# Attention scores by single heads and half tiles in quarters of TensorE's array, with first and second heads in separate PSUM banks

## The chip, the cores and the metric

One Trainium2 chip, one of its cores. The metric is the device time of one execution in microseconds (us). The kernel has an attention stage (about the first 147 us of the span) and behind it a mixture-of-experts stage; the change touches the attention stage alone.

## The reference, cut to what matters

```python
def _attn_ref(q, k, v):                       # 8 batches, 8 heads, 576 queries, 64 values a head
    k_p = k.reshape(B, H, Sp, 8, D).mean(axis=3)      # keys and values pooled by 8: Sp = 72
    v_p = v.reshape(B, H, Sp, 8, D).mean(axis=3)
    scores = scale * np.matmul(q, k_p.transpose(0, 1, 3, 2))
    scores = scores - np.max(scores, axis=-1, keepdims=True)
    attn = np.exp(scores)
    attn = attn / (np.sum(attn, axis=-1, keepdims=True) + 1e-09)
    return np.matmul(attn, v_p)
...
```

The result, 4608 rows of 512 numbers, goes through a gate to one of 8 experts (two layers, 512 to 1024 to 512) and is added to itself; rows that a skip score leaves out stay as they are.

## The kernel before, in words

**Tiling.** The 4608 queries are 36 tiles of 128. A batch has 576 queries, which are four and a half tiles, so four of the 36 tiles (t = 4, 13, 22, 31) hold 64 queries of one batch and 64 of the next. All eight heads of a tile are worked on together, as four pairs g. The queries lie as `qts[..][:, t % QG, g, :]`: 128 partitions, of which 0 to 63 are the 64 dimensions of the pair's first head and 64 to 127 those of its second, by 128 queries.

**Scores (`scores`, L299 to L305).** The pooled keys of a batch lie in `kbd`, for each pair a block-diagonal matrix of 128 partitions by 144: the first head's 72 keys stand in partitions 0 to 63 and columns 0 to 71, the second head's in partitions 64 to 127 and columns 72 to 143, and the rest is zero. `keys` (L213, ScalarE) writes it. One matmul of a pair (L303, queries as the weights, 144 moving columns, 128 rows deep) gives both heads' scores. `scores(t, half)` does pairs 0 and 1 into one PSUM bank, `scores(t, 1)` pairs 2 and 3 into a second one. A tile of two batches does each matmul in two halves of 64 queries, each with its own batch's keys. All of it is fp32, and the trace shows each such matmul as two weight loads and two matmuls ("passes" below; a transpose is one). There are three banks for scores (`ps_s`, L169), so a tile's second bank is the one that the tile before used first.

**Softmax.** `least` (L309, VectorE) takes, bank by bank, the smallest of each head's negated scores. `exped` (L315, ScalarE) makes the exponentials, one instruction per head, four for each bank, into `e`.

**Values.** `turn_p` (L323, L324) transposes `e` on TensorE into one PSUM tile `pt` of which there is one; `turned_p` (L328, ScalarE) copies it to `pT` in one instruction; `values` (L341, L344) multiplies by the values into `o`, of which there is also one; `normalised` (L355 to L362, VectorE) divides by the sum and writes the rows `x`, which go out by DMA, and the gate's logits.

**The order** is written out by hand, since the stage is under a manual schedule: each engine does its instructions in the order in which the program emits them. In step t of the loop (L842 to L896) the steps that matter here are, in this order: copy `pT` of tile t-2 (L848), for a new batch copy its transposed values (`turned_v`, L267), divide tile t-3 (`normal`), scores of tile t (L856), smallest scores (L861), for a new batch the gate's products (`gates_pe`, L278), in some steps the routing's products (L397 to L401), exponentials of t (L874), values of t-2 (L875), transposes of t-1 (L877). Weight splits on ScalarE and VectorE, sums of values on GpSimd, loads and indirect writes are put in between by planners with costs and due steps; none of these is touched.

**The start** (L819 to L840) does the scores and exponentials of tiles 0 and 1, then the sums of the first batch's values on VectorE (`first_sums`, L239), the transposes and the `pT` of both tiles, the first batch's gate products and the scores of tile 2. The keys of the first batch come pair by pair: the loop at L740 sums one pair's keys on VectorE (`sum_k`, L208) and writes its two blocks on ScalarE (L213), so that the first tile's matmuls follow pair by pair.

Of the kernel before, what the change touches and what calls it, by code (L numbers as in the profile page):

```python
# [26 lines left out]
F32 = mybir.dt.float32  # L27
# [3 lines left out]
AF = mybir.ActivationFunctionType  # L31
# [5 lines left out]
B, H, S, HD, POOL = 8, 8, 576, 64, 8  # L37
SP = S // POOL
# [44 lines left out]
QG = 2  # L83
KO = 128 - SP
KL = SP - KO
GAP = 2 * KL
# [77 lines left out]
def attention(tc, nc, q, k, vm, vr, cf, wg, w1, w2, whi, wlo, out, c, pay, offs, table, near, bufs, late, early, mb, fin, cfs):  # L164
    with ExitStack() as ctx:
# [3 lines left out]
        ps_s = pool("ps_s", 3, space=PSUM)  # L169
# [14 lines left out]
        kbd = [third[:, i * n:i * n + n].rearrange("p (g k) -> p g k", g=4) for i in range(2)]  # L184
# [9 lines left out]
        halves = [slice(hh * 64, hh * 64 + 64) for hh in range(2)]  # L194
        kts, kps, vts, vss, lss, vTs, qts = {}, {}, {}, {}, {}, {}, {}
# [9 lines left out]
        def sum_k(b, g):  # L205
            if b not in kps:
                kps[b] = kp.tile([128, 4, SP], F32, name="kp")
            nc.vector.tensor_reduce(kps[b][:, g], kts[b][:, g], axis=AX.X, op=ALU.add)  # L208
# [56 lines left out]
        def turned_v(b, tp):  # L265
            vTs[b] = vT = vp.tile([128, 3, 128], F32, name="vT", bufs=1)
            nc.scalar.activation(vT, tp, AF.Copy)  # L267
# [7 lines left out]
        def gates_pe(b):  # L275
            vT = vTs.pop(b)
            for j in range(3):
                nc.tensor.matmul(gp[:, j * 36:j * 36 + 36], vT[:, j, :], wgs[:, j * 36:j * 36 + 36], start=True, stop=True)  # L278

        def gates_dve(b):  # L280
            nc.vector.tensor_tensor(vbd[b % 2].rearrange("p g (h c) -> p g h c", h=2)[:, :, :, HD:VA - 1],
                                    gp[:, 0:72].rearrange("p (g h c) -> p g h c", g=4, h=2),
                                    pair.unsqueeze(3).broadcast_to([128, 4, 2, 9]), ALU.mult)
            nc.vector.tensor_tensor(vl4[b % 3][0:n4, :, HD:VA - 1], gp[:n4, 72:108].rearrange("p (g c) -> p g c", g=4),
                                    left.unsqueeze(2).broadcast_to([n4, 4, 9]), ALU.mult)
# [8 lines left out]
        def parts(t):  # L294

            b0, b1 = t * 128 // S, (t * 128 + 127) // S
            return [(slice(0, 128), b0)] if b0 == b1 else [(slice(0, 64), b0), (slice(64, 128), b1)]

        def scores(t, half):  # L299
            sc = ps_s.tile([128, 512], F32, name="sc")[:, 0:4 * SP]  # L300
            for g in range(2):
                for sl, b in parts(t):
                    nc.tensor.matmul(sc[sl, g * 2 * SP:(g + 1) * 2 * SP], qts[t // QG][:, t % QG, half * 2 + g, sl],  # L303
                                     kbd[b % 2][:, half * 2 + g, :], start=True, stop=True)
            return sc  # L305

        def least(sc, mn, i):

            nc.vector.tensor_reduce(mn[:, i * 4:i * 4 + 4], sc.rearrange("p (h k) -> p h k", k=SP), axis=AX.X, op=ALU.min)  # L309

        def exped(e, sc, mn, i):
            ev = e[:, (4 * SP + GAP) * i:(4 * SP + GAP) * i + 4 * SP].rearrange("p (k g) -> p g k", g=2)
            for h in range(4):
                k0 = (h % 2 ^ i) * SP
                nc.scalar.activation(ev[:, h // 2, k0:k0 + SP], sc[:, h * SP:(h + 1) * SP], AF.Exp,  # L315
                                     bias=mn[:, 4 * i + h:4 * i + h + 1], scale=-1.0)

        def turn_p(e):
            for i in range(2):
                k0 = (4 * SP + GAP + 2 * KL) * i  # L320
                ev = e[:, k0:k0 + 256].rearrange("p (k g) -> p g k", g=2)
                for g in range(2):
                    nc.tensor.transpose(ptf[:, (2 * i + g) * 128:(2 * i + g) * 128 + 128], ev[:, g], ident)  # L323
            nc.tensor.transpose(ptf[:, 512:640], e[:, 256:384], ident)  # L324

        def turned_p():
            pT = ap.tile([128, 5, 128], F32, name="pT")
            nc.scalar.activation(flat(pT), ptf[:, 0:640], AF.Copy)  # L328
            return pT

        def values(t, pT, apart=False):
            if apart:
                os = [ps_s.tile([128, 512], F32, name="sc") for _ in range(2)]
            else:
                o = ps_o.tile([128, 2, 512], F32, name="o")
                os = [o[:, 0], o[:, 1]]
            for a, o_ in enumerate(os):
                ov = o_[:, 0:4 * VA].rearrange("p (g h c) -> p g h c", g=2, h=2)
                for g in range(2):
                    for sl, b in parts(t):  # L340
                        nc.tensor.matmul(o_[sl, g * 2 * VA:(g + 1) * 2 * VA], pT[:, 2 * a + g, sl], vbd[b % 2][:, 2 * a + g, :],  # L341
                                         start=(g == 0), stop=False)
                for sl, b in parts(t):
                    nc.tensor.matmul(ov[sl, :, 1, :], pT[:, 4, sl], vl4[b % 3][:, 2 * a:2 * a + 2, :], start=False, stop=True)  # L344
            return [o_.unsqueeze(1) for o_ in os] if apart else [o]
# [250 lines left out]
        class Queue:  # L596
# [18 lines left out]
            def exponentials(self):  # L615
                if self.held is EXPS:
                    self.step(True)
# [119 lines left out]
        o = ps_o.tile([128, 2, 512], F32, name="o")  # L737
# [52 lines left out]
        scs, es, pts, os_ = {}, {}, {}, {}  # L790
# [6 lines left out]
        def normal(t):  # L797
            nrm = normalised(t, os_.pop(t))
            next(nrm)
            routes.step()  # L800
            finish(nrm)
            routes.step()
            add_routes(t + 1)

        def softmax(t, sc):
            mn = ap.tile([128, H], F32, name="mn")
            for i in range(2):
                least(sc[i], mn, i)
            return mn

        def exponentials(t, sc, mn):
            es[t] = ebuf[t % 2]
            for i in range(2):
                exped(es[t], sc[i], mn, i)

        def constant_product():
            nc.tensor.matmul(o[:, 0, :], init[:, 0:128], init[:, 0:512], start=True, stop=True)
# [1 line left out]
        for t in range(2):  # L819
            now["t"] = t  # L820
            for f in loads.pop(t, ()):
                f()
            sc = [scores(t, i) for i in range(2)]
            exponentials(t, sc, softmax(t, sc))
        constant_product()
        first_sums()
# [7 lines left out]
        sum_k(1, 1)  # L834
        gates_pe(0)
        gates_dve(0)
        sc = [scores(2, i) for i in range(2)]
        mn = softmax(2, sc)
        sum_k(1, 2)
        gps.take(1)  # L840
# [1 line left out]
        for t in range(2, NT):  # L842
            now["t"] = t
            for f in loads.pop(t, ()):
                f()
            new = turns.get(t)
            if t > 3:
                pts[t - 2] = turned_p()  # L848
            if t > NT - TILES:
                xhigh()  # L850
            if new is not None:
                turned_v(new, tp)
            routes.exponentials()
            if t > 2:
                normal(t - 3)
                sc = [scores(t, i) for i in range(2)]  # L856
            if t == NT - 1:
                turn_p(es.pop(t - 1))
                pts[t - 1] = turned_p()
            if t > 2:  # L860
                mn = softmax(t, sc)  # L861
            if t == 3:
                sum_k(1, 3)
            if new is not None:
                gates_pe(new)
            if t > NT - TILES:
                xlow()
            if t == NT - 1:
                while routes.step():
                    pass  # L870
            else:
                routes.products()
            spent = act.take(t, 0.4 if new is not None else 0.0, 1)
            exponentials(t, sc, mn)  # L874
            os_[t - 2] = values(t - 2, pts.pop(t - 2))  # L875
            if 2 < t < NT - 1:
                turn_p(es.pop(t - 1))  # L877
            if t >= NT - TILES:
                assert not later
                if t == NT - TILES:  # L880
                    tx, steps = tile_steps()
                xhigh, xlow = tx(bufs["ring"][:, t - NT + TILES], t - NT + TILES, ps_s.tile([128, 512], F32, name="sc"))
            if new is not None:
                gates_dve(new)
            for hh in range(2) if t in (2, 3) else ():
                keys(1, hh, slice(0, 3) if t == 2 else slice(3, 4))
            busy = dve.take(t, 0.25 if new is not None else 0.0)
            act.take(t, spent)
            while t < NT - 1 and busy < (DVE if t < PICKED else DVEL) and routes.step():
                busy += 0.24  # L890
            later.pop(t, lambda: None)()
            if t == FILLS:
                gps.fill = clear
            gps.take(t)
            if t + 1 in turns:
                tp = turn_v(turns[t + 1])  # L896
# [883 lines left out]
```

## Time and profile before

| what | us |
|---|---|
| median of 3 runs (482.95, 485.91, 1611.41) | 485.91 |
| profiled execution, its own time | 483.38 |
| span of that profile | 481.3 |
| TensorE matmul busy, weight loads busy | 464.6, 417.1 |
| VectorE, ScalarE, GpSimd busy | 304.0, 225.7, 247.9 |

The span runs from the first to the last instruction of the program; 2.1 us of the execution's time lie around it. One of the three runs is far from the other two, so the lower two, 3 us apart, are what the profiled execution is to be held against. TensorE's granted clock is full speed in all 40 slices.

### The profile page before, as it was taken

To read this page: it belongs to the slowest core of one execution; us is meant where nothing else is said; L and a number is where in the kernel's file an instruction comes from. 1 tells how busy PE (TensorE), PEld (TensorE's weight loads), DVE (VectorE), ACT (ScalarE), POOL (GpSimd) and SP (SyncE) were. 2 spreads that over 40 slices of the span, in tenths; PEclk is the share of its full clock that TensorE was granted. 3 is DMA by queue.
4 is the path that set the end of the run, shared out by engine and by line. 5 is a ranking of instruction groups with operands and counts; after the bars stand their busy time and mean duration, and the time that the engine had idled before them with its cause. 6 is when DMAs were issued, how large, how long until landed. Compare 5 with 4: busy or idle time off the path is not lost. (4 is left out here: it accounts for less than half of the span.)

```text
span 481.3 us, 11187 instructions
## 1 busy us (share of the span) xinstructions
PE 464.6 (97%) x3043; PEld 417.1 (87%) x3044; DVE 304.0 (63%) x713; ACT 225.7 (47%) x578; POOL 247.9 (52%) x328
## 2 busy tenths in 40 slices
PE   7999999999999999999999998999999999999995
PEld 3799899989999879898989986989899898989894
DVE  5877888798788622579795667662846655343321
ACT  4678778888891201545463645512435241212110
POOL 4498499999998054433343525153443161515242
PEclk9999999999999999999999999999999999999999
DMA  8999999996931025689787496877577323322021
GB/s 278 396 394 392 345 360 338 362 337 212 327 113 68 11 54 190 207 260 325 217 320 239 124 325 231 303 235 257 189 238 255 101 88 109 128 65 88 22 87 42
DMA packets 52042, 103.88 MB, mean 216 GB/s; under 512 B 10031, under 2 KB 22959, under 8 KB 50336
## 3 DMA queue, kind: packets, MB, share of 16 engines
q1 hardware_dynamic: 40544, 78.18, 47.8%
q0 software_dynamic: 11456, 25.22, 14.9%
q8 instruction: 17, 0.28, 0.2%
q14 instruction: 25, 0.20, 0.1%
HBM read 80.85 MB, written 31.21 MB: 233 GB/s over the span
## 5 line engine op out<-in xcount | busy, mean ns | idle before, releaser
L1288 POOL DMA_INDIRECT out<-ring,slot x33 | 34.9, 1057 | 107.3 <-POOLq L1114 103.9
L315 ACT ACTIVATE e<-sc,mn 128x72 f32<-128x72 f32 x288 | 65.0, 346 | 7.2 <-DVE mn L309 6.8
L1520 ACT ACTIVATE hhi<-psl 128x256 fp32r<-128x256 f32 (+3 forms) x59 | 23.5, 400 | 95.4 <-ACTq L1114 94.9
L1376 PE MATMUL psl<-xhi,w1hi 128*128 128x256 f32 (+3 forms) x220 | 64.1, 291 | 0.0
L1377 PE MATMUL psl<-xlo,w1hi 128*128 128x256 f32 (+3 forms) x220 | 64.1, 291 | 0.0
L1378 PE MATMUL psl<-xhi,w1lo 128*128 128x256 f32 (+3 forms) x220 | 64.0, 291 | 0.0
L1283 POOL DMA_INDIRECT ring<-out,slot x42 | 46.8, 1115 | 25.4 <-issue 25.4
L341 PE MATMUL o<-vbd,pT 128*128 128x148 f32 (+1 forms) x312 | 49.4, 298 | 1.1 <-DVE x L360 1.1
L1619 DVE SCALAR_TENSOR_TENSOR hlo<-psl,hhi 128x256 fp32r<-128x256 f32 (+2 forms) x55 | 23.3, 423 | 41.2 <-DVEq L1114 41.1
L415 POOL DMA_INDIRECT table<-pay,r_di x36 | 36.6, 1018 | 12.6 <-DVE mb L443 6.4
L1376 PEld LDWEIGHTS psl<-xhi,w1hi 128*128 128x128 f32 x220 | 41.3, 188 | 0.8 <-issue 0.4
L1377 PEld LDWEIGHTS psl<-xlo,w1hi 128*128 128x128 f32 x220 | 41.3, 188 | 0.5
L341 PEld LDWEIGHTS o<-vbd,pT 128*128 128x128 f32 (+1 forms) x312 | 38.6, 179 | 3.5 <-ACT ring L213 1.0
L1378 PEld LDWEIGHTS psl<-xhi,w1lo 128*128 128x128 f32 x220 | 41.2, 187 | 0.0
L1296 POOL DMA_DIRECT2D sorted<-ring x39 | 22.1, 567 | 33.3 <-DMA ring<-out,slot 27.4
L1596 DVE TENSOR_TENSOR w2lo<-stage,w2hi 128x1024 fp32r<-128x1024 f32 x28 | 34.4, 1228 | 6.9 <-DVEq L1114 6.8
L1377 PE MATMUL psd<-xlo,w1hi 128*128 128x256 f32 (+3 forms) x132 | 38.4, 291 | 0.0
L1376 PE MATMUL psd<-xhi,w1hi 128*128 128x256 f32 (+3 forms) x132 | 38.4, 291 | 0.0
L1378 PE MATMUL psd<-xhi,w1lo 128*128 128x256 f32 (+3 forms) x132 | 38.4, 291 | 0.0
L1402 PE MATMUL mb<-w2hi,hlo 128*128 128x512 f32 x88 | 34.8, 396 | 0.0
L1402 PE MATMUL psf<-w2hi,hlo 128*128 128x512 f32 x88 | 34.8, 396 | 0.0
L1400 PE MATMUL psf<-w2hi,hhi 128*128 128x512 f32 x88 | 34.8, 395 | 0.0
(276 smaller groups left out, 1214.7 us busy)
## 6 DMA issues: line engine op xcount, KB each, us to landing
stage<-in_w SPq DMA_DIRECT2D x64, 512.0 KB, 5.3
sorted<-ring POOLq DMA_DIRECT2D x39, 256.0 KB, 3.9
out<-x SPq DMA_DIRECT2D x36, 256.0 KB, 6.1
stage<-in_k SPq DMA_DIRECT2D x6, 1152.0 KB, 6.3
blocks<-sorted SPq DMA_DIRECT2D x100, 64.0 KB
qt<-in_q SPq DMA_DIRECT2D x9, 512.0 KB, 6.7
hhi<-in_vm SPq DMA_DIRECT2D x4, 1024.0 KB, 7.6
hlo<-in_vm SPq DMA_DIRECT2D x3, 1024.0 KB, 13.1
```

The costliest lines, as they stand in the source:

```text
L315: nc.scalar.activation(ev[:, h // 2, k0:k0 + SP], sc[:, h * SP:(h + 1) * SP], AF.Exp, bias=mn[:, 4 * i + h:4 * i + h + 1], scale=-1.0)
L341: nc.tensor.matmul(o_[sl, g * 2 * VA:(g + 1) * 2 * VA], pT[:, 2 * a + g, sl], vbd[b % 2][:, 2 * a + g, :], start=(g == 0), stop=False)
L415: m = nc.gpsimd.indirect_dma_start(table, bass.IndirectOffsetOnAxis(ap=di[:, j:j + 1], axis=0), flat(fin["pays"][:, t0 + j:t0 + j + TW // ...
L1283: g.indirect_dma_start(ring[:, (s + 3) % 9, 0:D], None, out, bass.IndirectOffsetOnAxis(ap=slot[:, s:s + 1], axis=0), bounds_check=NTOK - 1 ...
L1288: g.indirect_dma_start(out, bass.IndirectOffsetOnAxis(ap=offsets, axis=0), ring[:, (s + 3) % 9, 0:D], None, bounds_check=NTOK - 1, oob_is_ ...
L1376: t.matmul(ps, whi[0][:, k, w], xhi[:, k, xs], start=(k == 0), stop=False)
L1377: t.matmul(ps, whi[0][:, k, w], xlo[:, k, xs], start=False, stop=False)
L1378: last = t.matmul(ps, wlo[0][:, k, w], xhi[:, k, xs], start=False, stop=(k == 3))
L1400: t.matmul(ps, hhi[:, k, sl], whi[1][:, k, :], start=(k == 0), stop=False)
L1402: last = t.matmul(ps, hlo[:, k, sl], whi[1][:, k, :], start=False, stop=(k == 7))
L1520: a.activation(hhi[:, f, xs], bank(f, xs, alone), AF.Relu).then_inc(sem["act"], 1)
L1596: v.tensor_tensor(chunk_of(wlo, c), chunk_view(stage[c], c), chunk_of(whi, c).bitcast(F32), ALU.subtract).then_inc(sem["wlo1" if c < 4 els ...
```

## The change

The scores are made head by head. A matmul takes the 64 partitions `r` of one head (queries and keys), 64 of the tile's 128 queries (`sl`) and 72 moving columns: 16 matmuls per tile in place of 4 (of 8 in a tile of two batches). The four of one pair lie in the four quarters of the 128 by 128 array: two row halves by two column halves. The scores of the four first heads go to the first bank, those of the four second heads to the other. `exped` takes the heads in the order of the banks and writes each to the same place in `e` as before; the column of `mn` that belongs to a head follows. Both banks are taken before the first matmul, and the first pair writes both.

```diff
-        def scores(t, half):
-            sc = ps_s.tile([128, 512], F32, name="sc")[:, 0:4 * SP]
-            for g in range(2):
-                for sl, b in parts(t):
-                    nc.tensor.matmul(sc[sl, g * 2 * SP:(g + 1) * 2 * SP], qts[t // QG][:, t % QG, half * 2 + g, sl],
-                                     kbd[b % 2][:, half * 2 + g, :], start=True, stop=True)
+        def scores(t):
+            sc = [ps_s.tile([128, 512], F32, name="sc")[:, 0:4 * SP] for _ in range(2)]
+            for g in range(4):
+                for i, sl in enumerate(halves):
+                    b = (t * 128 + i * 64) // S
+                    for r, o in zip(halves, range(2)):
+                        nc.tensor.matmul(sc[o][sl, g * SP:(g + 1) * SP], qts[t // QG][r, t % QG, g, sl],
+                                         kbd[b % 2][r, g, o * SP:(o + 1) * SP], start=True, stop=True)
             return sc
...
-        def exped(e, sc, mn, i):
-            ev = e[:, (4 * SP + GAP) * i:(4 * SP + GAP) * i + 4 * SP].rearrange("p (k g) -> p g k", g=2)
-            for h in range(4):
-                k0 = (h % 2 ^ i) * SP
-                nc.scalar.activation(ev[:, h // 2, k0:k0 + SP], sc[:, h * SP:(h + 1) * SP], AF.Exp,
-                                     bias=mn[:, 4 * i + h:4 * i + h + 1], scale=-1.0)
+        def exped(e, sc, mn, o):
+            for g in range(4):
+                i = g // 2
+                ev = e[:, (4 * SP + GAP) * i:(4 * SP + GAP) * i + 4 * SP].rearrange("p (k g) -> p g k", g=2)
+                k0 = (o ^ i) * SP
+                nc.scalar.activation(ev[:, g % 2, k0:k0 + SP], sc[:, g * SP:(g + 1) * SP], AF.Exp,
+                                     bias=mn[:, 4 * o + g:4 * o + g + 1], scale=-1.0)
...
-            for i in range(2):
-                exped(es[t], sc[i], mn, i)
+            for o in range(2):
+                exped(es[t], sc[o], mn, o)
...
-            sc = [scores(t, i) for i in range(2)]
+            sc = scores(t)
```

The last replacement stands in three places: the start's loop over tiles 0 and 1, the scores of tile 2, and the main loop.

## Rows read from the trace of the kernel before

**Rows 1.** The page's first two parts: busy times; TensorE's tenths in 40 slices.

```profile
PE 464.6 (97%) x3043; PEld 417.1 (87%) x3044; DVE 304.0 (63%) x713; ACT 225.7 (47%) x578; POOL 247.9 (52%) x328
...
PE   7999999999999999999999998999999999999995
```

**Rows 2.** Timeline of one ordinary tile: start, duration, engine, line; idle before in brackets.

```profile
67.83 0.27 PE L324 MATMUL pt<-cfs,e 128*128 128x128 f32 x1
...
67.94 1.15 PE L303 MATMUL sc<-ring,qt 128*128 128x144 f32 x8
68.20 0.70 ACT L328 ACTIVATE pT<-pt 128x640 f32<-128x640 f32 x1 [0.59 <-PE pt L324]
...
68.70 0.88 DVE L309 TENSOR_REDUCE mn<-sc 128x4 f32<-128x288 f32 x2
68.95 0.55 PEld L341 LDWEIGHTS o<-vbd,pT 128*128 128x128 f32 x4
...
69.19 1.81 ACT L315 ACTIVATE e<-sc,mn 128x72 f32<-128x72 f32 x8 [0.29 <-DVE mn L309]
...
71.41 0.71 ACT L328 ACTIVATE pT<-pt 128x640 f32<-128x640 f32 x1 [0.40 <-PE pt L324]
```

**Rows 3.** Waits from 16 to 147 us: total us, times, longest.

```profile
ACT pT L328 <- PE pt L324: 14.8, 22, 1.4
...
DVE mn L309 <- PE sc L303: 2.5, 7, 0.6
...
PEld mb L278 <- ACT vT L267: 2.3, 5, 0.8
...
PEld mb L397 <- ACT ex L394: 1.2, 3, 0.7
```

**Rows 4.** Timeline: scores and values of tiles of two batches, in column halves.

```profile
57.13 0.32 PEld L303 LDWEIGHTS sc<-ring,xhi 128*64 128x64 f32 x6 [0.17 <-issue]
...
57.14 1.20 PE L303 MATMUL sc<-ring,xhi 128*64 128x144 f32 x16
...
66.14 0.29 PE L344 MATMUL o<-vl,pT 128*64 128x148 f32 x1
...
66.15 0.29 PE L344 MATMUL o<-ring,pT 128*64 128x148 f32 x1
...
66.27 0.29 PE L344 MATMUL o<-vl,pT 128*64 128x148 f32 x1
...
67.25 0.56 PEld L323 LDWEIGHTS pt<-cfs,e 128*128 128x128 f32 x4 [0.20 <-issue]
```

**Rows 5.** Groups by line and shape: L303's weight loads (busy us, mean ns).

```profile
L303 PEld LDWEIGHTS sc<-ring,qt 128*128 128x128 f32 x160 | 21.1, 191 | 3.8 <-ACT ring L213 2.5 <-issue 1.0 <-ACT e L315 0.2
...
L303 PEld LDWEIGHTS sc<-ring,xlo 128*64 128x64 f32 x32 | 2.0, 136 | 0.3 <-issue 0.3
```

**Rows 6.** Timeline of the start, from the last keys to the first values.

```profile
8.86 0.45 DVE L309 TENSOR_REDUCE mn<-sc 128x4 f32<-128x288 f32 x1
8.97 0.54 ACT L213 ACTIVATE ring<-kp 64x72 f32<-64x72 f32 x2 [0.51 <-DVE kp L208]
...
9.54 3.73 ACT L315 ACTIVATE e<-sc,mn 128x72 f32<-128x72 f32 x16
...
10.11 0.95 DVE L309 TENSOR_REDUCE mn<-sc 128x4 f32<-128x288 f32 x2 [0.81 <-PE sc L303]
...
10.55 0.54 PEld L303 LDWEIGHTS sc<-ring,qt 128*128 128x128 f32 x4 [0.20 <-ACT e L315]
...
13.06 0.79 ACT L328 ACTIVATE pT<-pt 128x640 f32<-128x640 f32 x1
...
13.90 0.56 PEld L323 LDWEIGHTS pt<-cfs,e 128*128 128x128 f32 x4 [1.13 <-ACT pT L328]
...
17.38 1.23 PE L303 MATMUL sc<-ring,qt 128*128 128x144 f32 x8
...
18.44 0.67 PE L341 MATMUL o<-vbd,pT 128*128 128x148 f32 x4
```

More of the change, by code (lines that the diff above doesn't have):

```diff
@@ L836, in attention @@
         gates_dve(0)
-        sc = [scores(2, i) for i in range(2)]
+        sc = scores(2)
         mn = softmax(2, sc)
@@ L855, in attention @@
                 normal(t - 3)
-                sc = [scores(t, i) for i in range(2)]
+                sc = scores(t)
             if t == NT - 1:
```

## The prediction, made before any run of the changed kernel

> **What bounds the kernel now.** I read the page first, then the timeline of one ordinary tile, then the waits of the stage, last the timeline of the start.
>
> The page makes TensorE look like the bound: 97% busy, nine tenths in nearly every slice [rows 1]. On that reading any TensorE time saved would come off the end. But busy TensorE includes matmuls that are merely early, so the stage has to be read tile by tile.
>
> One tile's loop [rows 2]: the last transpose starts at 67.83, the scores at 67.94; ScalarE copies pT from 68.20 to 68.90; the weight load for the values starts at 68.95, right behind that copy. The next pT copy starts at 71.41, 3.21 us after the first. So the loop runs: transposes, pT copy, values, transposes. The scores are not a link in it: they fill the 1.12 us (67.83 to 68.95) in which TensorE would otherwise stand waiting for pT. ScalarE has 0.40 us to spare ahead of the next pT, and it waits there for the transposes.
>
> The waits say how general that is [rows 3]: 22 times in the stage ScalarE waits for the transposes before pT. In tiles with a gate product or a routing product behind the scores, TensorE waits for ScalarE too (vT, ex), so there the scores lie under ScalarE's work as well. VectorE waits for scores only 7 times, 2.5 us in all.
>
> **The change part by part.**
>
> *Streaming.* Eight passes of 144 columns take 1.15 us, the last one 0.29 [rows 2, 4]: (1.15 - 0.29) / 7 = 0.123 us a pass, 0.98 us a tile. If the pitch goes with the columns, a pass of 72 takes 0.062. Its weight load has 64 columns; a load of 64 columns is 0.055 us shorter than one of 128 (136 against 191 ns [rows 5]), so a load should need some 0.055 and fit under that. A tile now has 16 matmuls of two passes, 32 passes. Bounds: all four quarters beside each other, 8 x 0.062 = 0.50 us; two at a time, 16 x 0.062 = 0.99; one by one, 32 x 0.062 = 1.98. The nearest row: a tile of two batches runs 16 passes in column halves in 1.20 us where 8 full ones take 1.15 [rows 4, 2], so two column halves run fully beside each other. Row halves are in no row; they read other partitions and write another bank, and I take them as independent too: 0.50 us.
>
> The Trainium skill, "TensorE: Matmul & The Clock Gate", section "The mechanism" of its part on packing small matmuls, says that matmuls start and end strictly in program order. The code issues the first half's product (vl, two passes) before the second half's (ring), yet ring's first pass starts 0.01 us after vl's first, and vl's second only at 66.27 [rows 4]: for column halves the trace does not bear the page out. By the page the second pass of each matmul would hold up the next matmul, and the block would come to 0.99 us; that is the first rival below.
>
> *Going in and out of the quarters.* Around a stretch of narrow matmuls the weight loads stand still for 0.17 us at the way in and 0.20 at the way out [rows 4]. Now every tile pays that around its scores, 32 tiles more than before. Bounds 0.2 to 0.37 per tile; I take 0.37.
>
> *Sum for an ordinary tile*, from the last transpose's start (T): first scores at T + 0.20, last pass at T + 0.20 + 0.06 (first load uncovered) + 7 x 0.062 = T + 0.69, free for the values at T + 0.89. pT lets the values go at T + 1.12. So the change costs nothing here and gains nothing: 0.23 us shorter on TensorE, all of it turned into a longer wait for pT. What covers it is the pT copy of 0.70 us with its way there and back; without that cover a tile would gain these 0.23.
>
> *Smallest scores and exponentials.* Before, the first bank is full half way through. Now both fill to the end: last pass T + 0.69 and about 0.25 to its result, T + 0.94 = 68.77 against a first minimum at 68.70 [rows 2]. Shift 0.1 us; behind it wait the exponentials and, on VectorE, sums and the division, but ScalarE has 0.40 us to spare before the next pT. Nothing. The exponentials' new order is the same eight instructions; transposes that read them come after the following tile's values. Nothing.
>
> *Banks.* A tile's second bank is freed by the first four exponentials of the tile before. It was needed half way through the scores and is now needed at once. Ordinary tile: exponentials from 69.19, four take 3 x 0.21 + 0.35 = 0.98 us ((1.81 - 0.35) / 7 = 0.21 apart), so free at 70.17, a microsecond before the next scores [rows 2]. Nothing.
>
> *The start*, where nothing covers it. The first bank of tile 0 was ready with two of four pairs (minimum at 8.86), so its exponentials began at 9.54, as soon as ScalarE had written the last keys at 9.51 [rows 6]. Now each bank needs all four pairs. The last keys at 9.51 with one pair's passes left to do: the banks are ready between 9.95 and 10.11 (where the second minimum began before); I take 10.0. Minimum 0.45, so exponentials start at 10.48, 0.94 late. They free their bank after 0.98, at 11.46; tile 1's scores wait for it (before: at 10.55, the row with the wait for ScalarE's e), now with nearly all of the tile behind that wait: 0.06 + 8 x 0.062 + 0.25 to the result, ready at 12.3; minimum 0.45, exponentials of tile 1 from 12.78, eight of them, 8 x 0.21 = 1.68 until pT may start at 14.4. Before, pT started at 13.06: 1.3 us late. From there to the values at 18.44 it is one chain without slack (pT, transposes waiting for pT, pT, gate product, scores, values): TensorE waits 1.13 for pT at 13.90 [rows 6]. VectorE's first value sums move as much. Bounds: 0.9 (tile 1's scores no later than tile 0's) to 1.8 (scores blocks of 0.99); nothing (the chain hidden behind the loads of the second batch) is the lower end. I take 1.3.
>
> *Where scores are on the path.* In the start the values of tile 0 follow the scores of tile 2 directly, 1.06 us after their first matmul (17.38, 18.44 [rows 6]). With the block at 0.06 + 7 x 0.062 and the way out at 0.20 it is 0.7, with the way in 0.9: -0.2.
>
> **Sum.** The experts' stage waits for the last tile's routing and then keeps TensorE at nine tenths or more [rows 1], so what the stage loses is taken to reach the end in full; if some is absorbed there, the result lies nearer to before. 483.38 (the profiled execution) + 1.3 - 0.2 = 484.5 us. That execution lies between the two close runs of the three shown; their median, 485.91, is 2.5 above it, more than the change. A measurement of this kernel can tell about 2% (9.7 us) from no change.
>
> **The rivals.**
>
> 1. *Row halves don't overlap, or passes keep program order.* The block is 16 x 0.062 = 0.99, the values may go at T + 0.20 + 0.06 + 15 x 0.062 + 0.20 = T + 1.39 instead of 1.12: 0.27 in each of 22 tiles that turn on pT, 5.9 us, and 1.8 at the start; where the later scores also delay exponentials up to 0.1 more a tile: 483.4 + 7.7 to 10 = 491 to 493.4. It decides from the point at which the block is longer than about 0.75 us. For it: no row shows row halves. Against: column halves overlap fully.
> 2. *Nothing overlaps once all quarters are in use.* 1.98 us; values at T + 2.38, 1.26 a tile over some 33 tiles, 42 us, and 3 at the start: 528, clearly slower. Against it the same rows.
> 3. *TensorE is the bound after all.* Each tile gains 0.23: 36 x 0.23 = 8 us, 475; if the ways in and out were free, 0.48 a tile, 17 us, 466, faster. For it: the page's 97%. Against it: the weight load of the values starts 0.05 after pT, not after the scores [rows 2].
> 4. *The start is covered and the rest gains a little*: 482 to 483. For it: loads of the second batch still come in at that time; against: TensorE and ScalarE wait for each other there, not for loads.
>
> **How the numbers follow.** Forecast (484.5, own range 483 to 486) 0.62; rival 4 0.14; rival 1 0.13, of which nearly half beyond 2%; rival 2 0.04; rival 3 0.07, of which half beyond 2%. Faster 0.04, within 2% 0.86, slower 0.10. The range, 481 to 492.5, leaves out rival 2, rival 3 and rival 1's upper end; its low side also holds run-to-run differences of the size of the two close runs.
>
> **What would show it.** Right: L303 as 32 passes a tile starting within 0.6 to 0.7 us, with idle weight loads around them; in ordinary tiles pT still 3.21 us apart and TensorE now waiting for pT ahead of L341; TensorE's busy share lower, the stage no shorter; at the start the first exponentials near 10.5 and the values of tile 0 near 19.7. Wrong: L303 blocks over 0.75 us, pT further than 3.21 apart in ordinary tiles (rivals 1, 2), or nearer than 3.1 (rival 3); or values of tile 0 still at 18.4 (rival 4).

## The result, and the profile after

| | executions | median us | lowest to highest |
|---|---|---|---|
| before | 19 | 483.26 | 480.81 to 488.40, one of 1611.41 |
| after | 19 | 485.62 | 484.44 to 490.06 |

After takes 1.0066 times as long as before, 95% interval 1.0043 to 1.0089: 2.1 to 4.3 us more. That is no change of 2%, and it is a small loss. The forecast of 484.5 is 1.1 us below the median of after and the range holds that median, but the loss that was forecast, 1.1 us, is about a third of the one that the ratio gives, 3.2 (2.4 between the medians). The base of the sum, the profiled execution of 483.38, was the right one: with 19 executions the median of before is 483.26, no longer 485.91.

The times of after are not one heap: twelve lie from 484.4 to 486.4, seven from 487.1 to 490.1. The profiled execution (485.25 us, span 483.4) is of the lower group, and one of only two of the 19 whose mean granted clock is 0.997 or more; this decides what its trace can tell. Ratios leave disturbed executions out; of e14_pairs_fill's twelve, below, these are six, from 491 to 494 us, so its median stands far above its ratio.

The page of after, against [rows 1]; the last line is the queue that brings TensorE its instructions (packets, MB, share):

```profile
PE 454.8 (94%) x3875; PEld 403.4 (83%) x3876; DVE 303.1 (63%) x713; ACT 225.9 (47%) x578; POOL 248.7 (51%) x328
...
PEclk9999999999999999999999999999999999999999
...
q8 instruction: 24, 0.39, 0.3%
```

TensorE is 9.8 us less busy and the span is 2.1 us longer, so the freed time was not on the path. It runs 832 more matmul passes. That the queue q8 brings TensorE's instructions is taken from its packets, which become more as TensorE's instructions do. The same queue on the page of before:

```profile
q8 instruction: 17, 0.28, 0.2%
```

The timeline of an ordinary tile, against [rows 2]:

```profile
35.02 0.27 PE L327 MATMUL pt<-cfs,e 128*128 128x128 f32 x1
...
35.22 0.58 PEld L305 LDWEIGHTS sc<-ring,xlo 64*64 64x64 f32 x32 [0.17 <-issue]
35.22 0.73 PE L305 MATMUL sc<-ring,xlo 64*64 64x72 f32 x32
35.38 0.70 ACT L331 ACTIVATE pT<-pt 128x640 f32<-128x640 f32 x1 [0.39 <-PE pt L327]
36.07 0.82 DVE L311 TENSOR_REDUCE mn<-sc 128x4 f32<-128x288 f32 x2 [0.23 <-PE sc L305]
...
36.14 0.77 PE L344 MATMUL o<-vbd,pT 128*128 128x148 f32 x4 [0.19 <-ACT pT L331]
36.56 1.80 ACT L318 ACTIVATE e<-sc,mn 128x72 f32<-128x72 f32 x8 [0.47 <-DVE mn L311]
...
38.59 0.70 ACT L331 ACTIVATE pT<-pt 128x640 f32<-128x640 f32 x1 [0.23 <-PE pt L327]
```

The 32 passes take 0.73 us where eight took 1.15, and the loop is as long as before: one pT copy follows the other after 3.21 us (35.38 to 38.59). The values start 1.12 us after the last transpose (36.14 - 35.02), as before. What is new is the bracket ahead of them: TensorE waits for ScalarE's pT. The waits of the stage (16 to 147 us), against [rows 3], say it of 17 tiles:

```profile
ACT pT L331 <- PE pt L327: 12.5, 21, 1.3
...
PE o L344 <- ACT pT L331: 3.6, 17, 0.4
```

The start, against [rows 6]:

```profile
8.16 0.55 ACT L213 ACTIVATE ring<-kp 64x72 f32<-64x72 f32 x2 [0.17 <-DVE kp L208]
...
9.15 0.82 DVE L311 TENSOR_REDUCE mn<-sc 128x4 f32<-128x288 f32 x2 [1.02 <-PE sc L305]
9.65 1.80 ACT L318 ACTIVATE e<-sc,mn 128x72 f32<-128x72 f32 x8 [0.94 <-DVE mn L311]
...
10.66 0.72 PE L305 MATMUL sc<-ring,qt 64*64 64x72 f32 x30 [1.54 <-ACT e L318]
...
17.92 0.73 PE L305 MATMUL sc<-ring,qt 64*64 64x72 f32 x32
18.58 0.77 PE L344 MATMUL o<-vbd,pT 128*128 128x148 f32 x4
```

Read alone, 18.58 against 18.44 looks as if the start had cost 0.14. But in this execution the last keys were written 0.80 us earlier (8.71 against 9.51). The exponentials start 0.94 behind the keys (before: 0.03), tile 1's scores wait 1.54 for them, and the values of tile 0 start 9.87 behind the keys instead of 8.93: the start is 0.94 longer. Where two executions are laid side by side, a chain has to be measured from the event that releases it.

The attention stage ends 0.34 later (last values 147.30 against 146.96). The rest of the 2.1 us of span came in one place of the experts' stage, of which this is the timeline of TensorE:

```profile
289.60 1.06 PE L1375 MATMUL mb<-plainx,plainw 128*128 128x128 f32 x8
292.56 2.92 PE L1375 MATMUL psd<-plainx,plainw 128*128 128x128 f32 x24 [1.91 <-PEq L1117]
```

From the first matmul of this line to the last it is 9.67 us here, 7.96 in the trace of before, 7.66 and 7.88 in the first two experiments, both with the same experts' stage, and 7.50 in r1_after_again, the same program: an accident of this execution, not of the change.

### The profile page after: what moved, and what is told of

Same layout as the page of the kernel before. It is cut to its first block, busy times and chain, and to the rows that moved or that the text cites. A ratio compares the mean times of both kernels' runs of the same rounds, so it can differ in the third digit from the quotient of the medians.

```text
span 483.4 us, 12857 instructions
## 1 busy us (share of the span) xinstructions
PE 454.8 (94%) x3875; PEld 403.4 (83%) x3876; DVE 303.1 (63%) x713; ACT 225.9 (47%) x578; POOL 248.7 (51%) x328
```

## The experiments

Each time is a median in us. "Start" is the time from the end of the last keys' write to the first values of tile 0; "stage" from the first to the last matmul of the values' first line.

| kernel | median | ratio to before beside it, interval | start | stage | clock in 9 to 16 us |
|---|---|---|---|---|---|
| before | 483.26 | | 8.93 | 128.40 | 1.00 |
| after | 485.62 | 1.0066, 1.0043 to 1.0089 | 9.87 | 128.60 | 1.00 |
| e1_start_pairs | 487.45 | 1.0094, 1.0059 to 1.0130 | 8.62 | 129.15 | 1.00 |
| e2_start_quarters | 486.08 | 1.0100, 1.0060 to 1.0141 | 11.74 | 128.51 | 0.52 |
| e3_half_scores | one run, other routing | | 11.13 | 128.33 | falls |
| e4_double_scores | 510.97 | 1.0565, 1.0526 to 1.0605 | 11.53 | 153.27 | falls |
| r1_after_again | 490.14 | 1.0136, 1.0096 to 1.0176 | 10.75 | 134.55 | falls in 12 to 16 |
| e8_warm_start | 485.05 | 1.0061, 1.0035 to 1.0087 | 9.88 | 129.22 | 1.00 |
| e9_cold_before | 486.68 | 1.0090, 1.0059 to 1.0122 | 11.34 | 129.89 | falls from 12 on |
| e5_split_after | 489.91 | 1.0129, 1.0093 to 1.0166 | 11.43 | 134.12, clock falls in it | falls |
| e11_warm_all | 485.47 | 1.0036, 1.0001 to 1.0072 | 9.88 | 129.51 | 1.00 |
| e12_before_half | 498.61 | other routing | 8.92 | 128.26 | 1.00 |
| e13_quarter_fill | 494.39 | 1.0253, 1.0185 to 1.0322 | 9.88 | 138.74 | 1.00 |
| e14_pairs_fill | 488.93 | 0.9996, 0.9952 to 1.0040 | 8.61 | 129.50 | 1.00 |

The experiments ran in three sets, each on a chip of its own and with executions of before beside it: e1 to e4; r1, e8, e9 and e5; e11 to e14. The same kernel after takes 1.0066 times as long as before in the first measurement and 1.0136 in r1_after_again, with intervals that don't overlap, so ratios are compared within a set.

### The start: pairs or quarters, one at a time

e1_start_pairs is the kernel after with tiles 0 and 1 made by the old `scores` and `exped`; e2_start_quarters is the kernel before with those two tiles made in the new way.

The first in the loop over tiles 0 and 1:

```diff
-            sc = scores(t)
-            exponentials(t, sc, softmax(t, sc))
+            sc = [scores_pairs(t, i) for i in range(2)]
+            mn, es[t] = softmax(t, sc), ebuf[t % 2]
+            for i in range(2):
+                exped_pairs(es[t], sc[i], mn, i)
```

The second in the same place of before:

```diff
-            sc = [scores(t, i) for i in range(2)]
-            exponentials(t, sc, softmax(t, sc))
+            sc = scores_quarters(t)
+            mn, es[t] = softmax(t, sc), ebuf[t % 2]
+            for o_ in range(2):
+                exped_quarters(es[t], sc[o_], mn, o_)
```

> The changed kernel with tiles 0 and 1 alone made as before (whole pairs, two pairs to a bank); quarters from tile 2 on. Start theory: the changed kernel loses 1.3 us at the start (first exponentials 0.94 us behind the last keys instead of 0.03, scores of tile 2 about 9.2 us behind the last keys instead of 7.9) and nothing in ordinary tiles. Then the scores of tile 2 come 7.8 to 7.9 us behind the last keys again, and the ratio to before falls from 1.0066 by 0.0027 to about 1.004; what is left would be a cost that is not in the start. Rival, all of the loss is the start and it is larger than 1.3: ratio 1.000. Rival, the loss is paid tile by tile (ways in and out of the quarters): ratio stays at 1.0066.

> The kernel before with tiles 0 and 1 alone made in quarters. Start theory: 1.3 us slower than before, ratio 1.0027, scores of tile 2 about 9.2 us behind the last keys; ordinary tiles as before. Rival, all of the loss is the start: ratio 1.0066. Rival, the loss is paid tile by tile: ratio 1.000.

In the traces the chain answers to the number. With pairs at the start and quarters from tile 2 on the start is 8.62 (e14_pairs_fill: 8.61); with quarters in all tiles and the clock at 1.00 it is 9.87 to 9.88 in four kernels. So quarters in tiles 0 and 1 cost 1.26, and quarters in tile 2, whose scores the first values follow, give back 0.31 (8.93 - 8.62).

The times do not answer to it. The ratios are 1.0094 and 1.0100 where 1.004 and 1.0027 were expected, e1's with four of six executions from 486.9 to 489.1 though its start is the old one. And in e2 the start is 11.74. With tile 2 in pairs its chain explains 8.93 + 1.26 = 10.19, so 1.55 us are left over. Its windows of the start (the third column from the right is the granted clock) show why:

```profile
0.00:9.00 9.00, 6.42 (x30) 2.85 (x31) 4.30 (x13) 3.08 (x9) 3.69 (x15) 1.00 0.78 255
9.00:16.00 7.00, 5.08 (x51) 3.53 (x49) 3.79 (x10) 4.15 (x18) 2.80 (x7) 0.52 1.04 372
```

TensorE's granted clock is at half, 1.2 GHz of 2.4, from about 9.3 to 16.2 us. Ahead of the fall it had stood waiting between the pairs (0.66, 0.19 and 0.37 us for the keys), and then it waited 1.54 for tile 0's exponentials. The scores of tile 1, the constants' products and the transposes then run at half speed. Before waits about as long between the pairs (0.37, 0.22 and 0.53) and keeps the clock in its trace; ahead of the fall e2 differs by the work between the waits, two rounds of four quarter passes a pair, 0.125 us of the array, for two passes of 0.123 each. This had not been in the prediction: the trace of before has 1.00 in every slice. Nor is it e2 alone: of the six traces with quarters in tiles 0 and 1 and no added product, five have such a fall (e2, e3, e4, e5 and r1_after_again, beginning between 8.7 and 12.2 us), all but the first trace of after.

### The clock at the start: keep it, or take its keeper away

In the start of both kernels stand three products of constants, on data that nothing reads, each where TensorE would otherwise wait. e8_warm_start is the kernel after with two more, e9_cold_before the kernel before without any of the three, and r1_after_again the kernel after once more, for a second trace.

e8, in `scores` behind a pair's matmuls, and in the start's loop behind the scores:

```diff
+                if t == 0 and g == 0:
+                    constant_product()
...
+            if t == 0:
+                constant_product()
```

e9, behind the start's first loop and in its second:

```diff
-        constant_product()
...
-            constant_product()
```

> The kernel after, unedited, for a second profile. Theory A (the chain alone: later exponentials and later second scores, some 1.3 us): the granted clock is 1.00 in 0 to 20 us as in the first profile, the values of tile 0 start near 18.6 to 19.8 us, and the time is some 1.3 above before in every run. Theory B (the chain, and in many runs also the clock: with less matmul work between the waits the granted clock falls to half within 9 to 17 us): the clock is below 0.9 in 0 to 20 us in a profile of the common kind, the values of tile 0 start near 21 us, and the median is 2.5 to 4 above before.

> The kernel after, with two more products of constants (each some 1.02 us of TensorE time on data that nothing reads): one behind the first pair of tile 0's scores, one behind all of tile 0's scores, both where TensorE stands waiting. Theory B (the clock): the clock stays at 1.00 in 0 to 20 us, the values of tile 0 start by 19.8, and the median lies 1.5 to 3 us below the kernel after, at 0 to 1.5 above before. Theory A (the chain alone): no better than the kernel after, since the work on the chain is the same or up to 0.3 longer; values of tile 0 as in the kernel after.

> The kernel before without the three products of constants that stand between the scores and the gate products of the start. Theory B: without them the clock of the kernel before falls too somewhere in 9 to 20 us; the values of tile 0 then start 1 to 3 us later than 18.44 and the median is 1 to 3 us above before. Theory A: some 0.5 us faster or the same, since 3 us of TensorE work in front of the transposes is gone; clock 1.00 throughout.

The second trace of after is of the common kind: 490.06 us, and its clock falls at the start and twice in the stage (windows; busy times, granted clock, DMA share, GB/s):

```profile
12.00:16.00 4.00, 4.00 (x12) 2.08 (x11) 3.86 (x9) 2.51 (x9) 0.76 (x2) 0.57 1.04 411
16.00:94.00 78.00, 69.92 (x1114) 62.06 (x1113) 61.20 (x194) 58.85 (x205) 60.62 (x73) 1.00 0.98 363
94.00:98.00 4.00, 4.00 (x24) 3.87 (x23) 2.23 (x12) 1.80 (x8) 3.68 (x4) 0.57 0.77 304
98.00:130.00 32.00, 27.35 (x459) 24.36 (x457) 26.24 (x78) 25.25 (x85) 28.00 (x39) 1.00 0.78 251
130.00:136.00 6.00, 5.54 (x65) 5.02 (x57) 3.30 (x14) 3.51 (x13) 5.47 (x7) 0.72 0.75 292
```

The median of r1_after_again is 7.4 above before beside it, where theory B had forecast 2.5 to 4: the falls in the stage were in neither theory.

With the two products the clock is 1.00 from 0 to 160 us in the trace, the start is the chain's 9.88, and the median is 5.1 below that of the same kernel without them, on the same chip (1.5 to 3 forecast), and still 2.3 above before (0 to 1.5 forecast). Over all executions: after has a mean clock of 0.997 or more in 2 of 25, with the products in 7 of 11, before in 39 of the 50 that ran beside the experiments. Those seven have a median of 484.30, 1.5 above before beside them (482.76); the four with a lower clock have 487.9.

Taking the three products out of before costs 3.9 us, in the traces 2.4 in the start and 1.5 in the stage, whose beginning the fall still covers; the windows show what they were for; first of e9_cold_before, then of before:

```profile
12.00:24.00 12.00, 9.35 (x39) 8.55 (x40) 6.81 (x16) 4.96 (x17) 5.22 (x7) 0.57 1.04 396
```

```profile
12.00:24.00 12.00, 10.84 (x75) 8.66 (x75) 10.21 (x24) 7.64 (x29) 5.73 (x7) 1.00 1.03 395
```

So theory B holds at the start: TensorE's work there was part of what kept the clock, and the change took some of it away. The Trainium skill, "TensorE: Matmul & The Clock Gate", section "HAM oscillation — how this bites in real kernels", describes a kernel whose matmuls run cold behind each wait for a DMA. The traces here show falls behind waits too, with 0.52 to 0.57 granted in the stretches of the start above, though TensorE waits there for keys and exponentials. That e8 did not bring all executions to before says that the stage has a loss of its own.

### The stage: is the gain covered?

e3_half_scores makes half as many quarter products, e4_double_scores makes each twice, e5_split_after lets the values start on a first part of pT.

e3, ahead of the matmul in `scores`:

```diff
+                        if t > 2 and g > 1:
+                            continue
```

e4, around the same matmul:

```diff
+                        for _ in range(2 if t > 2 else 1):
```

e5, in `turned_p`:

```diff
-            nc.scalar.activation(flat(pT), ptf[:, 0:640], AF.Copy)
+            for c0, c1 in (0, 512), (512, 640):
+                nc.scalar.activation(flat(pT)[:, c0:c1], ptf[:, c0:c1], AF.Copy)
```

> The changed kernel with the scores of the last two pairs left out from tile 3 on (8 matmuls a tile instead of 16; the smallest scores and exponentials read the first two pairs' instead, as many elements). The routing is then another, so only the attention stage is read, from the scores of tile 3 to the last tile's division. Cover theory: the scores block shrinks from 0.51 us to about 0.25 and the stage does not: pT copies stay 3.20 us apart in ordinary tiles and the stage from tile 3's scores to tile 35's keeps its 118.66 us within 0.5. Rival, TensorE is the bound: 0.25 us less a tile, some 8 us off the stage.

> The changed kernel with every score matmul issued twice from tile 3 on (64 passes a tile; the result is the same). The block grows from 0.51 to about 1.02 us. Cover theory: 0.23 to 0.3 us of that lie in the wait for pT, so an ordinary tile (22 of them) grows by 0.2 to 0.3 us and tiles with a gate product by nothing: 4.5 to 6.5 us over the changed kernel, ratio to before 1.016 to 1.020. Rival, TensorE is the bound: 0.51 us in each of 33 tiles, 17 us, ratio about 1.042.

> The kernel after with the copy of pT in two parts, columns 0 to 511 and 512 to 639, so that the values can start on the first. Cover theory (the freed 0.23 us of TensorE in an ordinary tile stand as a wait for pT): the values of an ordinary tile start up to 0.23 us earlier than 0.92 us after the first scores, the pT copies come 3.0 us apart instead of 3.2, and the stage is 3 to 5 us shorter than the 128.6 of the kernel after; the time 2 to 5 us below the kernel after. Rival (ScalarE, which has 0.4 us to spare in a tile and pays some 0.2 for the second copy, or the exponentials, becomes the bound): the copies stay 3.2 apart, stage 128 to 130 us, time within 1 us of the kernel after.

Taking another 0.25 us of scores out of each tile changes the stage by 0.27 us in all (128.33): the scores are off the path, as forecast. In e5 the values of an ordinary tile start 0.82 us behind the first scores instead of 0.92, and two pT copies are 3.10 apart instead of 3.20; the tiles with gate products that took 4.26 take 4.32. That is the cover again, worth 0.1 a tile when lifted and not 0.23; that the second copy takes the rest is likely but not shown. The time, 489.91, shows none of it under the clock's falls (mean clocks of 0.984 to 0.996); only tiles at full clock are read here.

e4 came out far above both expectations: 24.7 us more in the stage, 0.75 a tile, where the block's 0.51 less the 0.23 that were free would be 0.28. A part of it is the block itself: with the two copies of a matmul right behind each other, a block that nothing breaks off takes 1.16 us from its first pass to its last, not 1.02, so 0.42 a tile would be expected. And in the timeline of TensorE one block breaks off in the middle, for nothing that the profile shows:

```profile
30.18 1.02 PE L306 MATMUL sc<-ring,xhi 64*64 64x72 f32 x41
32.63 0.72 PE L306 MATMUL sc<-ring,xhi 64*64 64x72 f32 x23 [1.43 <-issue]
```

The matmul behind the gap has no semaphore to wait for. There are eleven such gaps in the stage, most of about 0.5 us. This named a second candidate: not how long TensorE works on the scores, but how many instructions it needs for them.

### The stage: idle time, or the number of instructions?

The edits begin with the fourth tile. e11_warm_all (on e8) and e14_pairs_fill (on e1) put one full-array product of constants behind each block, 0.22 us in two passes; e13_quarter_fill (on e8) fills 0.25 us with 16 more narrow passes; e12_before_half leaves TensorE as idle as the change does, with fewer instructions than before.

e11 and e14, behind the loops of `scores`:

```diff
+            if t > 2:
+                nc.tensor.matmul(banks[1][:, 4 * SP:4 * SP + 128], ident, ident, start=True, stop=True)
```

e13, in `scores`:

```diff
-            for g in range(4):
+            for g in (0, 1, 2, 3, 0, 1) if t > 2 else range(4):
```

e12, in `scores` of before:

```diff
-            for g in range(2):
+            for g in range(1 if t > 2 else 2):
```

> The kernel with the warm start, and in each tile from the fourth on one more full-array product of constants, 128 columns (0.22 us), behind the scores, into columns of the second score bank that nothing reads. Theory C (the freed TensorE time, left idle, lets the granted clock fall, at the start and in the stage): with 0.22 of the freed 0.46 us of a tile filled the clock falls less often; at most one execution in four has a mean clock below 0.997, and the median is 484 to 485, 1.1 to 2 above before, with no cluster at 487 to 489. Rival D (the clock falls in the stage for another reason, such as the narrow form of the score matmuls): mean clocks of 0.994 to 0.996 and times of 487 to 489 in nearly half of the executions, as with the warm start alone.

> The kernel with the warm start, and in each tile from the fourth on the quarter products of the first two pairs made twice, so that the score block is 0.25 us longer and the same TensorE time is filled as by the product of constants, but by quarter-array matmuls. Theory C, where idle time alone counts: as with the product of constants, clocks of 0.997 and more, median 484 to 485. Theory C with array use counting (narrow matmuls keep the clock up less): clocks below 0.997 and times of 487 to 489 in as many executions as without any filling.

> The kernel before with the scores of the second and fourth pair left out from the fourth tile on (the first pair's stand for them), which frees some 0.5 us of TensorE in a tile, as the change does, while every matmul keeps its full-array form. The routing and so the experts' work differ: only the clock and the stage are read. Theory C: TensorE waits for pT in every tile and the clock of the stage falls in some executions: mean clocks of 0.98 to 0.997 in several of them, where the kernel before has 0.995 to 1.00. Rival D: the clock stays at 0.995 to 1.00, and the stage at 128.4 us.

> The kernel after with tiles 0 and 1 made as before, and the product of constants of 128 columns behind the scores of each tile from the fourth on. Theory C: the chain of the start is as before and the clock holds: median within 1 us of before, clocks of 0.997 and more, values of tile 0 near 18.5. Rival D: the upper cluster stays, median 486 to 488 as without the filling.

The pair e11 and e13 is the sharp one: nearly the same TensorE time added to a tile, and the clock at 1.00 in both stages, but 129.51 us in one and 138.74 in the other, which neither version of theory C had forecast. Of e13's 9.2 us more, some 2.0 are gaps inside the blocks without any wait, such as this one ahead of a block's last pass, and 1.7 more waits inside blocks for a new batch's keys:

```profile
84.14 1.06 PE L305 MATMUL sc<-ring,qt 64*64 64x72 f32 x47
85.58 0.22 PE L305 MATMUL sc<-ring,qt 64*64 64x72 f32 x1 [0.38 <-issue]
```

Another 3.1 show on VectorE (late signals of 6.3 us against e11's 3.2, counted below), and 2.4 I can't place: the smallest scores start late although the block has been issued in time.

The two kernels differ in one more thing than the number of instructions. e13's repeats write the score banks anew, so the smallest scores wait for them; e11's product only follows. In one tile of each, first of e13, then of e11, the minimum starts 1.10 and 0.85 us behind the first pass:

```profile
67.71 1.05 PE L305 MATMUL sc<-ring,xlo 64*64 64x72 f32 x48
...
68.81 0.82 DVE L313 TENSOR_REDUCE mn<-sc 128x4 f32<-128x288 f32 x2 [0.30 <-PE sc L305]
```

```profile
69.07 0.73 PE L306 MATMUL sc<-ring,qt 64*64 64x72 f32 x32
...
69.92 0.82 DVE L316 TENSOR_REDUCE mn<-sc 128x4 f32<-128x288 f32 x2 [0.22 <-PE sc L306]
```

These 0.25 us in every tile are a rival of the number of instructions for part of the 9.2, and no run separates the two. The waits of VectorE for the scores, 22 to 148 us, of before, after, r1_after_again and e13_quarter_fill (total us, times, longest); e12_before_half has no such row:

```profile
DVE mn L309 <- PE sc L303: 2.2, 6, 0.6
```

```profile
DVE mn L311 <- PE sc L305: 4.0, 9, 0.7
```

```profile
DVE mn L311 <- PE sc L305: 8.1, 14, 1.4
```

```profile
DVE mn L313 <- PE sc L305: 17.6, 23, 1.8
```

One of them in r1_after_again:

```profile
87.52 0.73 PE L305 MATMUL sc<-ring,xhi 64*64 64x72 f32 x32
...
88.44 0.77 PE L344 MATMUL o<-vbd,pT 128*128 128x148 f32 x4 [0.19 <-issue]
89.08 0.33 SPq L292 DMA_DIRECT2D xhi<-in_q  x1
89.11 0.82 DVE L311 TENSOR_REDUCE mn<-sc 128x4 f32<-128x288 f32 x2 [0.69 <-PE sc L305]
```

In the ordinary tile above the minimum starts 0.85 us behind the first pass; here it is 1.59. Two engines were waiting for the block's signal, and both go on at the same moment (SyncE's load at 89.08, VectorE at 89.11), when TensorE has long been in the values. In the trace the semaphore that both wait for is counted up at 89.02 and 89.06: the signal came late, not the engines. Counted against the last pass of the block plus the usual 0.28, such late signals add up to 0 in before and e12, 0.4 in the first trace of after, 2.5 to 3.4 in e1, e8, e11 and e14, 5.8 in r1_after_again and 6.3 in e13 (7.5 with one wait that the view puts down to a routing product). In e3, with half the passes of after, they add up to 2.0, and its stage is not longer than before's. In e1, e8 and r1 the first four hit the same tiles, though the starts of these kernels differ; in e11 and e14, with two more passes in each tile, they hit other tiles, the same in both. So where they come, the place goes with the position in TensorE's instruction order; but the first trace of after, the same program as r1, has the tiles of r1 in time.

What the filling did to the clock: with it 9 of e11's 12 executions have 0.997 or more (7 of 11 without), and the median is 1.8 above before beside it, within what theory C forecast; but three executions of 487.9 to 495.0 remain, where theory C forecast no such group, so it became rarer at most. e12 stayed at 1.00 in the stage's windows with all that idle time, so idle time alone did not bring the clock down there; its four mean clocks (0.989 to 0.998) hold a fall at 256 to 262 us in its own experts' stage and decide nothing.

e14, with the old start and filled waits, fits the sum but does not close it. Its ratio of 0.9996 compares the six executions from 483.2 to 486.8; the other six lie from 491.1 to 494.2, higher than either theory forecast, and no trace shows why. Its stage is 1.1 longer than before's at full clock.

What stays open is what delays the signals. The queue that brings TensorE's instructions carries 17 packets in before, 24 in after, 28 in e13 and 32 in e4, in the order of the losses, and it shares the DMA engines, which are busy for 0.85 to 0.88 of this stage. But in no trace do the packets' times line up with every gap, and no kernel changed the number of instructions and nothing else, so the narrow form of the matmuls remains a rival too. The Trainium skill, "Runtime: NRT & Kernel Launch", section "Instruction fetch mechanics", says that instructions are fetched ahead in blocks of 16 KiB and that the cost of crossing from one to the next is mostly hidden; the packets here are of that size (0.39 MB in 24), and if e13's gaps come from there, it is not hidden in this stage. That it is the fetch is argued, not shown.

## Why the prediction was right or wrong

- *Streaming, way in.* Right: the last of 32 passes starts 0.51 behind the first (0.50 forecast), all four quarters run beside each other, and the weight loads stand for 0.17 at the way in. Rival 1 and rival 2 fall with it; row halves do overlap.
- *Ordinary tile.* Right: 3.21 us, the freed time stands as a wait for pT, though in 17 tiles, not 22. Rival 3 falls. e3 confirms the cover from the other side.
- *Smallest scores, banks.* The shift forecast as 0.1 is about 0.2 (the minimum 1.05 us behind the last transpose, 0.87 in [rows 2]), and hidden, as forecast. Wrong is that the minimum follows the last pass by a fixed quarter of a microsecond: in some tiles the signal is 0.3 to 1.3 us late. The stage is 0.2 us longer than before's in the first trace of after and 0.7 to 1.1 in e1, e8, e11 and e14, all at full clock; that the late signals make these differences is argued, and e3 has 2.0 us of them without a longer stage. No step of the prediction looked at what 832 more passes cost besides their time in the array.
- *The start*, 1.3 forecast. Right as a chain: first exponentials 0.94 behind the last keys, 1.26 for the tiles 0 and 1 in quarters. Wrong as a price: it was taken for the whole. With TensorE waiting between less work, its clock falls to half there in five of six traces, and the start gets 0.9 (r1_after_again) to 1.7 us (e4_double_scores) longer than the chain. The trace of before shows three products of constants at exactly this place, and a clock of 1.00; the prediction read both and did not ask what the kernel would lose if the clock did not hold.
- *Scores on the path at the start.* -0.2 forecast, -0.31 measured.
- *Rival 4*, the covered start: wrong, though the first trace of after, with its early keys, looks like it.
- *Sum.* +1.1 forecast. At full clock it is +1.5 (the seven executions of e8: 0.95 at the start, the rest in the stage), measured over all it is +2.1 to +4.3. The missing part is mainly the clock: at the start in five of six traces, in the stage in some (r1_after_again, e5). The step that failed is the start's term, 1.3, mis-sized because it held the clock constant: the start's chain is 1.26 at full clock, and 2.1 to 2.9 with the fall. The smaller part is the stage, which was put at nothing and is 0.2 to 0.8 longer at full clock without the filling products (after, e1, e8); its cause stays open. How the loss of the 19 executions divides between the two can only be estimated, since a mean clock doesn't tell where the clock fell.

## What to carry to other kernels

Here matmuls on quarters of the array ran fully beside each other, but a shorter block is worth nothing where TensorE only fills the wait for another engine; ask first what would start earlier. Work that hides in such a wait can still have a job: at the start of this kernel it held the clock. When such work is taken out, put something in its place or price the stretch at half clock. Cutting one matmul into four multiplies TensorE's instructions, and near a stage with busy DMA engines that number may have a price of its own; here that is argued, not shown.

## What the runs showed of the hardware that was not expected

- Passes of four fp32 matmuls on the four quarters start 6 to 7 ns apart, and a round of four takes 0.0625 us for 72 columns each: the array time of one.
- Three products of about 1.02 us, on data that nothing reads, are worth 3.9 us to this kernel: 2.4 in the start, 1.5 in the stage behind it (e9_cold_before).
- Sixteen more narrow passes in a tile cost 0.29 us a tile where TensorE had 0.23 us free; two wide passes of about the same length cost 0.01 (e13 and e11 against e8, over 33 tiles). The narrow ones also hold up the smallest scores by 0.25 us, so not all of it is their number.
- The signal of a finished block can reach the waiting engines up to 1.3 us late while TensorE is already at work on the next products.
